# Halved loads for two more pairs, and a new order of all steps, in a fused linear-attention and gated-MLP kernel

## The chip, the cores and the metric

The kernel runs on one core of a Trainium2 chip. The metric is the device time of one execution in microseconds (us); lower is better. A core has five engines that run side by side: TensorE (PE in the profile) multiplies matrices, VectorE (DVE), ScalarE (ACT) and GpSimd (POOL) work on elements, and SyncE (SP) issues most transfers between the chip's main memory and the on-chip memory. TensorE writes to PSUM, a memory of eight banks. Each engine takes its instructions strictly in the order in which they were written.

## The reference

Inputs are `q`, `k`, `v`, `f_logit` of shape (4, 8, 768, 48) and two weight matrices (384 x 2048 and 2048 x 384), all in float32.

```python
f = 1.0 / (1.0 + np.exp(-f_logit))
for t in range(S):                       # S = 768
    state = f[:, :, t, :, None] * state + np.einsum('bhd,bhe->bhde', k[:, :, t], v[:, :, t])
    y[:, :, t] = np.einsum('bhd,bhde->bhe', q[:, :, t], state)
x = y.transpose(0, 2, 1, 3).reshape(3072, 384)
h = x @ w_in
out = (h * np.cos(h)) @ w_out
```

## The kernel before

The 3072 tokens are cut into 12 *pairs* of 256 tokens, three for each of the four batches. The recurrence is computed in chunks: within a chunk as masked scores, between chunks through a 48 x 48 state of each head. Each pair is a small graph of *steps*, named by kind, pair and part:

- `f k q v`: loads, issued by SP. A pair in `HALVES` loads f, k and q as two halves of four heads each (`f0.0`, `f0.1`, 192 KB apiece); any other pair loads them whole (384 KB). `w0.j` and `w1.j` load quarters of the two weight matrices (768 KB), and `wc` casts them to bfloat16.
- `ex ln cum eb ei`: the gate. ACT forms log(1 + exp(-f)), PE sums it over the tokens with a triangular matrix (`cum`), and ACT takes exp of the sums with both signs (`eb`, `ei`).
- `qm km`: q and k times these decays; `tq tk qkt`: their transposes, on PE with a copy out of PSUM by DVE or ACT (pairs 0 to 3), or as a transposing transfer by SP (pairs 4 to 11).
- `vb vt`: v as bfloat16, and a second copy of it laid out for the output blocks.
- `sc am`: scores on PE, and the mask on DVE. `ps st si sz`: the state's sum, its carry, and its decay. `y yi xe`: the output from scores and from the state, and its copy out of PSUM.
- `zX.i`: zeroing of a buffer. `zf0` and up: matmuls on a tile of zeros, which compute nothing that is used; their number is `ZEROS`.

Two neighbouring tokens share one partition, as the even and the odd *parity*. In a whole pair, POOL first adds the two parities' logarithms (`ad`), so that `cum` needs one sum for both, and corrects for the even parity afterwards with a separate gate: ACT makes it (`fx`, `fy`), and POOL multiplies it into q and k (`qa`, `ka`). In a pair of `HALVES`, `ln` writes both parities as bfloat16, and `cum` (L386) sums over both on PE with two masks, `incl` and `strict`, for each half of the heads; `ad`, `fx`, `fy`, `qa` and `ka` do not exist there, and `ex`, `ln`, `cum`, `eb` and `ei` exist once for each half:

```python
for z in xe:
    for x in xe:
        nc.tensor.matmul(o[:, :, HB * z:HB * z + HB], lhsT=strict if x > z and cut else incl,
                         rhs=w[:, x, :, 0:D].rearrange("p (u h) d -> p u h d", u=un),
                         start=(z == 0 and x == 0), stop=False)
```

The MLP runs over units of 256 tokens, one for each pair: `h` (first product, L634, in eight half steps of six matmuls that fill two PSUM banks each with its twin), `co` (cosine on ACT, L639), `g` (product on DVE, L616), `o` (second product, L650, four steps for each 128 tokens), `ot` (copy out of PSUM) and `out` (store).

Nothing decides the order at run time. The string `ORDER` lists every step in one sequence that a planner wrote ahead of time, each with an engine letter (T TensorE, S ScalarE, V VectorE, G GpSimd, Y SyncE) and the buffer slots or PSUM banks that it takes: `h0.10:T0` is the first half step of block 1 of unit 0, on TensorE, in the banks from 0 on. `emit` writes the steps in that sequence, and each engine gets its part of it as its queue. Semaphores between the engines follow from the data and from the reuse of slots and banks.

Of the kernel before, what the change touches and what calls it, by code (L numbers as in the profile page):

```python
# [55 lines left out]
tq3.1:T6 w1.1:Y2 tk3.1:T qkt3.1:S2 ka2:G qkt3.0:V3 o2.2:T1 g1.3:V o1.2:T7 km2.1:G0 v2:Y1 o0.2:T0
wc1.0:S km2.0:G o3.2:T6 w1.3:Y4 sc3.0:T2 sc3.1:T4 qa2:G am3.0:V0 o0.0:T f4:Y2 o3.0:T qm2.1:G
am3.1:V2 vb3:S2 o2.0:T qm2.0:G tk2.1:T2 vt3.3:S0 tq2.1:T tk2.0:T3 qkt2.1:V4 f5:Y1 tq2.0:T ps3.0:T4,5
qkt2.0:V0 ps3.1:T wc1.1:G o1.0:T sz3.01:V0 sc2.0:T2 sz3.00:V k5:Y0 am2.0:V1 vb2:G0 o3.1:T o2.1:T
vt2.2:S2 vt3.1:G vt3.2:G ps2.1:T4 ps2.0:T sc2.1:T2 k4:Y2 st2.00:V wc1.3:G o0.1:T am2.1:V3 o1.1:T  # L60
st3.10:V v4:Y2 vt2.1:G o1.3:T ex4:S st3.11:V vt2.0:G o3.3:T ot1:V0 ln4:S1 vt2.3:G q4:Y1 o0.3:T
sz2.00:V3 ex5:S st2.01:V ad4:G2 o2.3:T sz2.01:V fx4:S ot3:V1 q5:Y2 ln5:S0 vt3.0:G cum4:T4 ot2:V2
y2:T2,3 ei4:S2 yi2:T ad5:G2 fy5:S yi3:T6 f9:Y0 y3:T1 xe2.0:V2 fx5:S ka4:G xe2.1:V fy4:S cum5:T7
sz3.10:V1 ei5:S0 h2.11:T2 sz3.11:V ka5:G out2:Y eb5:S2 xe3.1:V1 h2.10:T eb4:S0 xe3.0:V km4.1:G2
h2.21:T6 ot0:V3 v5:Y1 h2.01:T4 km4.0:G co2.1:S2 h2.00:T h3.21:T0 qa4:G co2.0:S3 g2.1:V1 h3.20:T
f6:Y2 qm4.0:G h2.20:T co3.2:S1 g2.0:V h2.31:T2 qm4.1:G co2.2:S0 h2.30:T g3.2:V3 vb4:G2 tq4.1:Y0
h3.11:T4 co2.3:S2 qa5:G g2.2:V h3.10:T h3.31:T0 vt4.2:S0 vt4.3:G f7:Y1 g2.3:V co3.1:S3 h3.30:T
vt4.0:G km5.1:G0 o5.1:T7 co3.3:S1 g3.1:V tq4.0:Y1 o4.0:T6 qm5.1:G o5.2:T g3.3:V q6:Y0 qm5.0:G
ps4.0:T4,5 sc4.1:T2 ps4.1:T o5.3:T st4.00:V ex6:S vb5:G0 tq5.1:Y4 st4.01:V o4.1:T sz4.01:V3 km5.0:G
ln6:S0 sz4.00:V o5.0:T out1:Y st4.11:V zsz.2:G fx6:S o6.3:T0 am4.1:V2 k6:Y2 ex7:S vt5.1:G2 o6.1:T  # L70
vt5.3:G tq5.0:Y3 ln7:S1 st4.10:V ps5.1:T1 ad6:G1 ps5.0:T sc4.0:T2 sz4.10:V2 o4.2:T am4.0:V3 fx7:S
zqk.1:G v6:Y2 o4.3:T vt4.1:S vt5.0:G ot5:S0 cum6:T4 sz4.11:V ad7:G2 ot4:S2 yi4:T2,3 st5.01:V ei6:S0
y4:T sz5.01:V1 eb6:S1 vt5.2:G sc5.1:T6 st5.00:V xe4.1:S2 xe4.0:V cum7:T5 o6.2:T out4:Y am5.1:V1
# [699 lines left out]
```

## Time and profile before

| | |
|---|---|
| time, median of 3 runs | 179.11 us (179.11 to 179.7) |
| profiled execution | 179.25 us |
| span, first to last instruction | 177.4 us |
| busy: PE / DVE / ACT / POOL | 168.1 / 134.3 / 128.9 / 106.3 us |
| matmuls on zeros | 28, 9.8 us of PE's busy time |
| first matmul of the MLP | 23.95 us |
| last copy out of PSUM starts | 174.20 us |

The span runs from the program's first instruction to its last; what the profiled execution's own time has beyond it lies around the program. A busy share counts every instruction of an engine, the matmuls on zeros among them, so it is to be read together with what the instructions do. In group rows, the figures after the bar are the group's busy time, the mean duration of one instruction in ns, and the idle time of the engine just before them, with what ended it.

### The profile page before, as it was taken

What the parts mean: (1) busy time and instruction counts of PE and PEld (TensorE: products, weight loads), DVE (VectorE), ACT (ScalarE), POOL (GpSimd) and SP (SyncE); (2) the same over time, 40 slices, a digit from 0 to 9 for tenths busy, and PEclk for the clock granted to TensorE, in tenths of its full rate; (3) what the DMA queues carried; (4) which work ended last, traced back from release to release, by engine and by line L of the source; (5) the groups of instructions that cost most, each with busy time, mean ns of one, the idle gap of its engine ahead of it and who ended that gap; (6) DMA issues with size and microseconds to landing.
All of it is one profiled execution on the core that took longest, in us unless ns stands there. A gap on an engine that the chain in (4) does not pass through costs nothing.

```text
span 177.4 us, 5663 instructions
## 1 busy us (share of the span) xinstructions
PE 168.1 (95%) x2402; PEld 121.8 (69%) x2402; DVE 134.3 (76%) x201; ACT 128.9 (73%) x179; POOL 106.3 (60%) x134
## 2 busy tenths in 40 slices
PE   2897999999999999999999999999999999999992
PEld 0454678966678866788668786668866876888661
DVE  6139897989886999979798878677578897685721
ACT  3778898895769999889998879968855460485401
POOL 5245899999769999779767993529796000000000
PEclk9999999999999999999999999999999999999999
DMA  5999999999944699996999996976009602210103
GB/s 137 321 323 370 351 378 372 285 366 322 252 137 108 147 260 232 262 299 147 231 242 263 315 155 154 204 199 193 0 0 167 166 0 89 81 60 0 44 4 133
DMA packets 74394, 34.45 MB, mean 194 GB/s; under 512 B 67457, under 2 KB 72833, under 8 KB 74369
## 3 DMA queue, kind: packets, MB, share of 16 engines
q1 hardware_dynamic: 73024, 33.50, 72.3%
q10 hardware_dynamic: 1344, 0.59, 1.1%
q8 instruction: 19, 0.31, 0.8%
q14 instruction: 7, 0.05, 0.1%
HBM read 25.17 MB, written 4.72 MB: 168 GB/s over the span
## 4 chain that ended last, share of the span: by engine, by line
PE 85%; DVE 7%; POOL 3%; ACT 3%; issue 1%; POOLq 0%; DVEq 0%
PE ps L650 36%; PE ps L634 34%; PE ps L572 5%; PE ps L472 4%; PE ps L386 2%; PE ps L512 2%; DVE qk L416 2%; PE ps L451 1%; DVE qkt L196 1%; DVE incl L217 1%; ACT bj L403 1%; DVE sz L544 1%; PE ps L277 1%; DVE x L196 1%; DVE am L494 1%
## 5 line engine op out<-in xcount | busy, mean ns | idle before, releaser
L616 DVE TENSOR_TENSOR g<-ps,co 128x1024 bf16<-128x1024 f32 x48 | 57.8, 1222 | 15.4 <-ACT co L639 13.4
L650 PE MATMUL ps<-w_out_bf,g 128*128 128x384 bf16 x384 | 67.3, 326 | 0.0
L634 PE MATMUL ps<-x,w_in_bf 128*128 128x256 bf16 x576 | 66.3, 273 | 0.2 <-DVE x L196 0.2
L639 ACT ACTIVATE co<-ps,halfpi 128x1024 bf16<-128x1024 f32 x48 | 52.7, 1113 | 16.9 <-PE ps L634 13.0
L634 PEld LDWEIGHTS <-w_in_bf 128*128 128x128 bf16 x576 | 55.5, 98 | 8.5 <-issue 0.4
L650 PEld LDWEIGHTS <-g 128*128 128x128 bf16 x384 | 36.2, 98 | 22.4 <-DVE g L616 0.2
L494 DVE TENSOR_TENSOR am<-ps,pmask 128x1024 bf16<-128x1024 f32 x24 | 28.6, 1218 | 5.8 <-PE ps L472 4.5
L416 POOL TENSOR_TENSOR qk<-k,bi 128x384 bf16<-128x384 f32 x20 | 19.8, 1000 | 0.6
L416 POOL TENSOR_TENSOR qk<-q,b 128x384 bf16<-128x384 f32 x20 | 19.7, 999 | 0.7
L373 POOL TENSOR_TENSOR sp<-ls 128x384 bf16<-128x384 f32 x10 | 10.0, 998 | 13.3 <-ACT ls L346 7.1
L196 POOL COPY vt<-vb 64x384 bf16<-64x384 bf16 x32 | 16.0, 501 | 2.6 <-ACT vb L196 1.0
L196 ACT COPY ot<-ps 128x384 f32<-128x384 f32 (+1 forms) x10 | 4.5, 461 | 12.7 <-PE ps L650 6.9
L544 DVE TENSOR_TENSOR sz<-ps,b 64x192 bf16<-64x192 f32 x32 | 11.3, 354 | 1.3 <-PE ps L512 0.4
L196 DVE COPY ot<-ps 128x384 f32<-128x384 f32 (+1 forms) x16 | 8.1, 514 | 5.5 <-PE ps L650 5.5
L360 POOL TENSOR_TENSOR k<-k,f 128x384 f32<-128x384 f32 x10 | 10.0, 1002 | 3.4 <-ACT ot L196 3.3
L538 DVE TENSOR_TENSOR ps<-ps,sz 64x192 f32<-64x192 f32 x28 | 10.3, 366 | 1.8 <-PE ps L512 0.8
L342 ACT ACTIVATE f<-f 128x768 f32<-128x768 f32 (+1 forms) x14 | 10.3, 746 | 1.0 <-DMA f<-in_f_logit_dram 0.8
L277 PE MATMUL ps<-zero 128*128 128x512 bf16 x28 | 9.8, 445 | 1.2 <-DVE zero L203 1.2
L350 POOL TENSOR_TENSOR q<-f,q 128x384 f32<-128x384 f32 x10 | 10.0, 1000 | 1.3 <-ACT f L353 1.3
L196 ACT COPY vt<-vb 64x384 bf16<-64x384 bf16 x16 | 8.1, 508 | 2.4 <-POOL vb L196 2.1
L472 PE MATMUL ps<-qkt 48*64 48x128 bf16 (+1 forms) x320 | 8.8, 219 | 0.7 <-DVE qkt L196 0.6
L196 POOL CAST vb<-v 128x768 bf16<-128x768 f32 x8 | 6.6, 824 | 4.7 <-DMA v<-in_v_dram 3.4
(66 smaller groups left out, 167.9 us busy)
## 6 DMA issues: line engine op xcount, KB each, us to landing
v<-in_v_dram SPq DMA_DIRECT2D x12, 384.0 KB, 4.9
out_dram<-ot SPq DMA_DIRECT2D x22, 192.0 KB, 3.3
f<-in_f_logit_dram SPq DMA_DIRECT2D x10, 384.0 KB, 5.1
k<-in_k_dram SPq DMA_DIRECT2D x10, 384.0 KB, 5.6
q<-in_q_dram SPq DMA_DIRECT2D x10, 384.0 KB, 5.7
g<-in_moe_w_in_dram SPq DMA_DIRECT2D x4, 768.0 KB, 8.8
g<-in_moe_w_out_dram SPq DMA_DIRECT2D x4, 768.0 KB, 7.2
q<-in_q_dram SPq DMA_DIRECT2D x4, 192.0 KB, 3.7
```

Of the source, the lines that this page charges most:

```text
L196: (nc.scalar.copy if e == "ACT" else eng(e).tensor_copy)(out=o, in_=i)
L277: G.step(f"zf{i}", ("PE",), lambda e, dump=dump: nc.tensor.matmul(dump.ap, lhsT=zero[:, 0:128], rhs=zero, start=True, stop=True), writes=[ ...
L342: nc.scalar.activation(out=flat(t.ap), in_=flat(t.ap), func=AF.Exp, scale=-1.0)
L416: G.step(f"{nm}{n}.{u}", ("POOL", "DVE") if cut else ("POOL",), lambda e, u=u, j=j, src=src, dec=dec: eng(e).tensor_mul(out=qkp[u][j].ap[: ...
L472: nc.tensor.matmul(o[t0:t1, r, 2 * a + g, :].rearrange("p (e n) -> p e n", e=2), lhsT=wide[s, t0 // 64, :] if turned else wide[s].rearrang ...
L494: G.step(f"am{n}.{u}", ("DVE",), lambda e, u=u, sc=sc: nc.vector.tensor_mul(out=am[u].ap.rearrange("p r b n -> p (r b) n"), in0=sc.ap.rear ...
L538: nc.vector.tensor_add(out=view()[s], in0=view()[s], in1=S0.ap[s, :, r, :])
L544: eng(e).tensor_mul(out=new.ap[s, :, r, :].rearrange("p (u a) n -> p u a n", u=2), in0=view()[s].rearrange("p (u a) n -> p u a n", u=2), i ...
L616: nc.vector.tensor_mul(out=o.rearrange("p b (n e) -> p b n e", e=2), in0=ph.ap.rearrange("p (b e n) -> p b n e", e=2, n=64), in1=co.ap.rea ...
L634: nc.tensor.matmul(ph.ap[:, i * T:(i + 1) * T].rearrange("p (g t) -> p g t", t=C), lhsT=w_in_bf[:, kk, f0:f0 + 128], rhs=xa[:, :, kk, :], ...
L639: G.step(f"co{m}.{j}", ("ACT",), lambda e, ph=ph, co=co: nc.scalar.activation(out=co.ap, in_=ph.ap, func=AF.Sin, bias=halfpi), reads=[ph], ...
L650: nc.tensor.matmul(po.ap[:, 0:DM], lhsT=gT.ap[:, j, i * C:(i + 1) * C], rhs=w_out_bf[:, j, :], start=(po.first and j == 4 * s), stop=(po.f ...
```

## The change

Three things are edited: two constants and the whole of `ORDER`.

- `HALVES` goes from pairs 0, 1 to pairs 0, 1, 2, 3. Pairs 2 and 3 lose `ad`, `fx`, `fy`, `qa` and `ka`; their `ex`, `ln`, `cum`, `eb`, `ei` and the loads of f, k and q come in two halves. Steps `qm` and `km` of these pairs may run on DVE as well as on POOL.
- `ZEROS` goes from 28 to 17.
- `ORDER` is a new plan of all 904 steps (909 before). Engines, slots and banks of steps are chosen anew too. `f0.0` and `f0.1`, which ACT issued, are issued by SP, the former as the very first load; `f0.1` is the third.

```diff
-HALVES = (0, 1)
+HALVES = (0, 1, 2, 3)
-ZEROS = 28
+ZEROS = 17
-f1.1:Y2 f0.1:S1 zf0:T5 v0:Y0 f0.0:S zf1:T0 q0.0:Y1 zqk.2:G k1.1:Y1 zqk.0:G zvt.2:G k0.0:Y2 ex1.1:S
-zsp.2:V zsz.0:V f1.0:Y ln1.1:S2 zvt.0:V zsp.1:V cum1.1:T2 k0.1:Y zf2:T3 q0.1:Y ei1.1:S0 vb0:G0
-zf3:T1 ex0.1:S zf4:T4 f2:Y0 ex0.0:S vt0.2:G0 zf5:T6 ln0.0:S1 eb1.1:S0 cum0.0:T0 v1:Y1 ln0.1:S zf6:T5
-zf7:T7 ei0.0:S1 zf8:T6 zf9:T6 cum0.1:T7 km0.0:G0 zf10:T4 f3:Y1 ei0.1:S zf11:T3 eb0.0:S1 zsz.3:G
-tk0.0:T4 zf12:T6 eb0.1:S vt0.3:G km0.1:V ps0.0:T2,0 vt0.1:S k1.0:Y ex1.0:S ps0.1:T zf13:T6 sz0.00:V0
-q1.1:Y0 vt0.0:S zf14:T6 zf15:T3 sz0.01:V zf16:T5 q1.0:Y st0.11:V zf17:T1 tk0.1:T6 ex2:S km1.1:V2
-zf18:T1 w0.1:Y0 qm0.0:V tk1.1:T3 ln2:S1 zf19:T7 qm0.1:V tq0.0:T zf20:T5 vb1:S1 qkt0.0:V2 w0.0:Y3
-ad2:G1 ln1.0:S sz0.11:V3 sc0.0:T4 tq0.1:T st0.10:V zsz.1:G ex3:S cum2:T2 am0.0:V1 w0.2:Y1 cum1.0:T7
-vt1.1:G2 zf21:T1 ei1.0:S vt1.2:G zf22:T1 zf23:T1 ei2:S1 qkt0.1:V0 zf24:T4 km1.0:G zf25:T5 eb1.0:S
-sz0.10:V ln3:S0 sc0.1:T6 ps1.1:T0,4 am0.1:V0 zf26:T1 eb2:S0 k3:Y2 ad3:G1 ps1.0:T fx3:S si1.0:T
-tk1.0:T1 fx2:S qm1.0:V yi0:T5 qm1.1:G y0:T6 sz1.01:V1 tq1.0:T xe0.1:S2 cum3:T7 sz1.00:V w0.3:Y2
-xe0.0:S qkt1.0:V0 tq1.1:T fy2:S zf27:T2 wc0.1:G qkt1.1:V1 eb3:S1 sc1.0:T0 ei3:S0 am1.0:V3 yi1:T3,2
-vt1.0:S sc1.1:T6 q3:Y2 si1.1:T vt1.3:G am1.1:V0 h0.10:T0 wc0.0:S h0.11:T sz1.10:V1 sz1.11:V y1:T
-w1.2:Y4 h0.01:T6 xe1.1:V0 wc0.2:G xe1.0:V h0.00:T co0.1:S3 k2:Y1 h1.01:T2 ka3:G h1.21:T4 fy3:S
+f0.0:Y0 zf0:T0 v0:Y0 zf1:T3 f0.1:Y zqk.2:G k0.0:Y0 f1.1:Y1 f1.0:Y q0.0:Y0 ex0.0:S zsz.2:V zvt.2:V
+k0.1:Y zsp.2:V zvt.0:V ln0.0:S2 zqk.1:V q0.1:Y vb0:G1 cum0.0:T5 q1.1:Y1 ex0.1:S vt0.0:G2 zf2:T4
+f3.1:Y2 ln0.1:S zf3:T0 vt0.2:G ei0.0:S0 f2.1:Y0 zf4:T2 eb0.0:S0 km0.0:V2 cum0.1:T1 k1.1:Y1 ex1.1:S
+zsp.1:V tk0.0:T3 v1:Y0 eb0.1:S qm0.0:G zf5:T4 zf6:T2 ei0.1:S zf7:T5 ex1.0:S km0.1:V zsz.0:G k1.0:Y
+tq0.0:T ln1.1:S2 ps0.0:T2,5 qkt0.0:V1 ln1.0:S q1.0:Y cum1.1:T0 vt0.3:G zsz.3:V zf8:T6 vt0.1:S f2.0:Y
+qm0.1:V ps0.1:T ei1.1:S0 zf9:T7 w0.1:Y2 tk0.1:T1 sz0.01:V2 ex3.1:S cum1.0:T7 sz0.00:V eb1.1:S1
+tq0.1:T zf10:T6 st0.11:V ei1.0:S f3.0:Y zf11:T0 qm1.1:G2 st0.10:V zf12:T4 ex2.1:S sz0.10:V0 w0.0:Y0
+ln2.1:S2 sz0.11:V tq1.1:T4 ln3.1:S1 km1.1:V sc0.0:T2 km1.0:G w0.2:Y4 qkt0.1:S0 zf13:T0 am0.0:V0
+cum2.1:T5 tk1.1:T eb1.0:S zf14:T6 w0.3:Y1 zf15:T0 vb1:S2 qkt1.1:V2 sc0.1:T6 qm1.0:G zf16:T2 am0.1:V3
+ei2.1:S1 tk1.0:T1 ps1.0:T4,3 ex2.0:S ps1.1:T vt1.2:G0 si1.0:T eb2.1:S0 tq1.0:T vt1.3:G sz1.01:V3
+yi0:T2 ln2.0:S y0:T0 sz1.00:V qkt1.0:V0 sc1.1:T6 xe0.1:S2 q3.0:Y2 wc0.1:G xe0.0:S am1.1:V2 sc1.0:T4
+q3.1:Y ex3.0:S cum2.0:T2 cum3.1:T1 ln3.0:S am1.0:V0 vt1.1:G h0.10:T6 ei2.0:S w1.2:Y3 eb2.0:S vt1.0:G
+si1.1:T cum3.0:T0 ei3.1:S0 sz1.11:V2 wc0.0:G y1:T4,5 ei3.0:S sz1.10:V yi1:T eb3.0:S1 h0.11:T eb3.1:S
+xe1.0:V1 k3.1:Y2 xe1.1:V h0.01:T0 zqk.0:V wc0.2:G h0.00:T k2.0:Y0 co0.1:S3 h1.01:T4 k3.0:Y h1.00:T
+co0.0:S2 g0.1:V4 wc0.3:G h1.21:T2 w1.0:Y2 co1.0:S0 h1.20:T g0.0:V qm3.0:G0 h1.11:T6 q2.1:Y0 h1.10:T
...
```

More of the change, by code (lines that the diff above doesn't have):

```diff
@@ L56 @@
[L56 to L73, printed above, removed]
@@ L115 @@
-ot21:S2 out21:Y
+f0.0:Y0 zf0:T0 v0:Y0 zf1:T3 f0.1:Y zqk.2:G k0.0:Y0 f1.1:Y1 f1.0:Y q0.0:Y0 ex0.0:S zsz.2:V zvt.2:V
[3 more added lines that the diff above has]
+tq0.0:T ln1.1:S2 ps0.0:T2,5 qkt0.0:V1 ln1.0:S q1.0:Y cum1.1:T0 vt0.3:G zsz.3:V zf8:T6 vt0.1:S f2.0:Y
@@ new lines @@
+h1.31:T2 km3.1:G co0.3:S3 h0.20:T v2:Y2 tk3.1:T6 g0.3:V km3.0:G co0.2:S0 h1.30:T tq3.0:T7 zsz.1:G
+tk3.0:T co1.3:S2 g0.2:V tq3.1:T k2.1:Y o3.2:T4 wc1.0:G qkt3.1:S3 o2.2:T5 f4:Y1 g1.3:V o0.2:T1
+qkt3.0:S1 km2.0:G2 o0.0:T qm2.0:V v3:Y1 o1.2:T0 qm2.1:G sc3.0:T2 sc3.1:T6 wc1.1:S am3.0:V0 o3.0:T
+w1.3:Y3 o1.0:T vb2:G2 am3.1:V2 f5:Y0 o2.0:T vt2.1:G0 o3.1:T km2.1:V vt2.0:G q4:Y0 tq2.0:T6 ex4:S
+tk2.0:T tk2.1:T2 qkt2.0:V4 tq2.1:T o1.1:T vt2.3:S v4:Y0 qkt2.1:V2 vb3:G1 ln4:S0 sc2.0:T6 am2.0:V3
+vt3.3:G2 ps3.1:T3,2 ps3.0:T fy4:S o0.1:T vt3.1:S k4:Y2 sz3.00:V1 o2.1:T wc1.3:G vt3.2:S sz3.01:V
@@ L116 @@
+out21:Y
 """
```

99 lines of the change are left out of this document (55 added, 44 removed).

## The prediction

> **What bounds the kernel now.** I read the page first (span, busy shares, chain), then the busy time by stretches, then the chain in order of time, then the start instruction by instruction. The page, with its shares of the chain by engine:
>
> ```profile
> span 177.4 us, 5663 instructions
> PE 168.1 (95%) x2402; PEld 121.8 (69%) x2402; DVE 134.3 (76%) x201; ACT 128.9 (73%) x179; POOL 106.3 (60%) x134
> PE 85%; DVE 7%; POOL 3%; ACT 3%; issue 1%; POOLq 0%; DVEq 0%
> ```
>
> TensorE is busy for 95% of the span, but part of that is filler on the tile of zeros. The stretches (length, then busy time of PE, PEld, DVE, ACT, POOL) and the chain in order of time (start, length) say where it does needed work; the first of these rows are the matmuls on zeros alone, the next three are all instructions:
>
> ```profile
> 0.00:10.00 10.00, 4.23 (x10) 0.94 (x10) 0.27 (x1) 1.00 0.90 240
> 10.00:20.00 10.00, 5.17 (x18) 1.42 (x17) 0.00 (x0) 1.00 1.10 357
> 25.98:174.20 148.22, 147.93 (x2089) 109.64 (x2088) 117.36 (x159) 108.67 (x143) 90.70 (x108) 1.00 0.70 175
> 11.03:25.05 14.02, 12.51 (x243) 7.99 (x241) 12.82 (x22) 12.85 (x25) 9.36 (x11) 1.00 1.08 358
> 6.39:23.06 16.67, 14.95 (x243) 8.85 (x244) 10.83 (x20) 14.14 (x31) 10.05 (x14) 1.00 1.10 347
> ...
> 23.95 1.47 PE ps L634 x12
> 25.42 0.56 PE ps L572 x32
> 25.98 9.28 PE ps L634 x84
> ...
> 174.20 0.48 ACT ot L196
> ```
>
> Read this as three parts. From 25.98 us, where step h0.01 starts (h0.10, h0.11 and y1 come just before it), to 174.20 us PE stops for only 148.22 - 147.93 = 0.29 us. The tail, from 174.20 to 177.4, is 3.2 us of copy and store. The first 26 us are the filling of the pipeline: DVE is busy for 12.82 of 14.02 us there, ACT for 14.14 of 16.67, and PE's apparent load is padded with 9.4 us of zeros. So only the first part can become shorter, and the middle can only keep its 0.29 us of stalls or get more.
>
> Call A the time at which h0.01 starts. In both orders the same 266 TensorE steps stand from h0.01 to the end, and ahead of it the same steps but for the sums of pairs 2 and 3 and the fillers. With an unchanged middle, the end moves by exactly what A moves.
>
> **The change part by part.** The durations that I use (group rows: busy, mean ns), then the moments of the start:
>
> ```profile
> L342 ACT ACTIVATE f<-f 128x768 f32<-128x768 f32 x10 | 8.4, 838 | 0.1
> L346 ACT ACTIVATE sp<-f 128x384 bf16<-128x384 f32 x4 | 2.1, 519 | 0.1
> L403 ACT ACTIVATE bj<-ps 128x384 f32<-128x384 f32 x4 | 2.0, 490 | 2.8 <-PE ps L392 2.8
> L356 ACT ACTIVATE f<-ls 128x384 f32<-128x384 f32 x10 | 5.1, 521 | 0.1
> L196 ACT CAST vb<-v 128x768 bf16<-128x768 f32 x4 | 3.3, 824 | 0.0
> L196 ACT COPY qkt<-ps 128x1024 bf16<-128x1024 bf16 x1 | 1.0, 1003 | 0.0
> L494 DVE TENSOR_TENSOR am<-ps,pmask 128x1024 bf16<-128x1024 f32 x24 | 28.6, 1218 | 5.8 <-PE ps L472 4.5 <-PE ps L572 1.2
> L196 DVE COPY qkt<-ps 128x1024 bf16<-128x1024 bf16 x7 | 4.7, 684 | 0.4 <-PE ps L451 0.4
> L544 DVE TENSOR_TENSOR sz<-ps,bb 64x192 bf16<-64x192 f32 x8 | 2.8, 353 | 0.6 <-PE ps L512 0.5
> L416 POOL TENSOR_TENSOR qk<-q,b 128x384 bf16<-128x384 f32 x20 | 19.7, 999 | 0.7
> L196 POOL CAST w_in_bf<-g 128x1536 bf16<-128x1536 f32 x3 | 4.4, 1461 | 0.1
> ...
> 3.96 0.52 ACT L342 ACTIVATE f<-f 128x384 f32<-128x384 f32 x1 [0.80 <-DMA f<-in_f_logit_dram]
> 5.83 1.87 PE L277 MATMUL ps<-zero 128*128 128x512 bf16 x4
> 8.85 0.49 ACT L403 ACTIVATE bj<-ps 128x384 f32<-128x384 f32 x1 [0.18 <-PE ps L392]
> 12.11 1.25 PE L277 MATMUL ps<-zero 128*128 128x512 bf16 x5
> 16.35 0.33 PE L386 MATMUL ps<-sp,incl 128*128 128x384 bf16 x1
> 16.62 0.24 PE L386 MATMUL ps<-sp,incl 128*128 128x192 bf16 x1
> 17.05 1.37 PE L277 MATMUL ps<-zero 128*128 128x512 bf16 x5
> 24.83 1.28 ACT L639 ACT_TABLE_LOAD   x1
> 26.12 1.11 ACT L639 ACTIVATE co<-ps,halfpi 128x1024 bf16<-128x1024 f32 x1
> ```
>
> *Pairs 2 and 3 by halves.* Removed per pair: three POOL products (ad, qa, ka), 3 x 1.0 us, so 6 us in all; POOL is idle 40% of the span and ends no part of the middle, so I count nothing. On ACT, ex and ln as wholes (0.84 each), fx and fy (0.52 each), one ei and one eb (0.49 each), 3.7 us, become four halves of 0.52 and four of 0.49, 4.0 us: +0.3 us per pair, in the start. On PE one whole sum took 16.35 to 16.62 = 0.27 us; a half with both parities 16.62 to 17.05 = 0.43, so 0.86 per pair: +1.2 us for both. They stand before A, where 11 fillers go (0.25 us each by 12.11's row), 2.8 us; the cover is PE's idle time there. If that were gone, they would cost 1.2. DVE gets two of the products qm, km (about 0.6 each) in the middle, where it is busy for 117 of 148 us: nothing.
>
> *Loads.* The bytes stay; 200 KB pieces replace wholes, and SP issues 9 more entries (f +4, k +2, q +2, out +1), among them f0.0 and f0.1 that ACT issued before. Moved past SP's queue, f0.1 lands third. The landings below are issue time plus time to landing, in the order: first two f halves (issued at 0.74), second f half and v0 (1.25), k0.0 (3.1), w0.0 (12.9).
>
> ```profile
> DMA to landing us min/median/max: 3.2/3.4/3.5
> DMA to landing us min/median/max: 4.9/5.0/5.1
> DMA to landing us min/median/max: 4.9/4.9/4.9
> DMA to landing us min/median/max: 8.1/8.1/8.1
> ```
>
> So 384 KB had landed at 4.25 us, 960 at 6.3, 1536 (with k0.0) at 8.0, and w0.0, byte position 5376 KB, at 21.0. In the new order f0.1 ends at 768 KB: by interpolation 5.6 us (an estimate). q0.0 takes the place of 1536 KB: 8.0 us. w0.0 stays at 5376 KB: 21.0. Two entries can hold SP up: f2.1 needs f0.1 read by ln0.1 (6.7 below) and v1 needs v0's slot free (cast before 7 us); both are issued about 4 us before they land, as the rows show, so the loads in flight cover that.
>
> *The new order up to A.* ex0.0 starts at 3.96 as now, waiting for the same first load. ex0.1 and ln0.1 follow f0.1: 5.6 + 2 x 0.52 = 6.7; ei0.0 ends at 7.1 to 7.2, where it ended at 8.85 + 0.49 = 9.34 before. qm0.0 (POOL, 1.0) waits for q0.0: 8.0 to 9.0. Then tq0.0, ps0.0, cum1.1 on PE, some 1.4 us with fillers, and ei1.1, ex3.1, eb1.1 on ACT (1.5): eb1.1 ends at 12.0, or 12.8 if no ACT instruction overlaps the one before. qm1.1 on POOL (1.0), then tq1.1 and sc0.0 on PE (0.8 with the handoffs): am0.0 starts at 14.0 to 14.9. From here DVE is a straight row of am0.0, qkt1.1, am0.1, sz1.01, sz1.00, qkt1.0, am1.1, am1.0: 4 x 1.22 + 2 x 0.68 + 2 x 0.35 = 6.9 us, plus up to 0.5 of waiting for sc0.1: 20.9 to 22.4. y1 and yi1 then take 0.9 us and h0.11 0.66 (6 x 9.28/84): A by this path is 22.5 to 24.0.
>
> Two other conditions hold h0.01. It takes PSUM banks 0 and 1, which hold cum3.0 and cum3.1 until eb3.0 and eb3.1 have read them, and these are the last of 35 ACT instructions from ex0.1 on. Their durations add to 18.4 us (14 x 0.52, 16 x 0.49, vt, vb, qkt, two xe). In the stretch 6.39:23.06 ACT ran 29 instructions whose own durations add to 16.2 in 14.14 us, so overlap saves 13%: 16.0 us. From 5.6 that is 21.6 without a wait and 24.2 with the 2.5 us of waiting of that stretch. And it needs wc0.0: 21.0 + 1.46 = 22.5. So A lies between 22.5 and 24.65 (24.0 or 24.2 plus late handoffs); I take 23.7, just past the middle, because three paths meet there. That is 2.3 us earlier than 25.98.
>
> *After A.* Banks come free through co and g. Before, the first co started at 26.12; now the table load (1.28) and co0.1 (1.11) follow eb3.1, which ends near 22.9: 25.3. PE needs that bank six half steps (3.9 us) after A, at 27.6, and g0.1 ends at about 25.3 + 1.3 = 26.6: it fits. Pair 3's k comes late in the queue: behind w0.0 (21.0) stand w0.2, w0.3, q3, w1.2 and k3.1, 2880 KB, at the 358 GB/s of the stretch 11.03:25.05 some 8.2 us, so it lands near 29.2, k3.0 1.1 later, and POOL forms km3.1 and km3.0 by 31.6; PE asks for them at A + 8.5 = 32.2. That is little slack, so I give the middle 0.4 us more stalls than its 0.29 (bounds: -0.29, and +1.5, five times the present sum).
>
> *Tail and ends.* The last steps are the same copy and store by ACT and SP: 3.2 us. One store moves from ACT to SP, off the last chain: nothing.
>
> *The sum.* 23.7 + 148.2 + 0.4 + 3.2 = 175.5 us of span. The profiled execution took 179.25 for 177.4, so 1.85 lies around the span: 177.35; it was 0.14 above the median, 179.11. Forecast **177.2**.
>
> **A rule that speaks against it.** The four fillers at 5.83 took 0.47 us each, the five at 12.11 0.25: PE runs at about half speed until some 10 us, though the clock column reads 1.00. With 11 fillers fewer it could fall back. Were it slow for the first 3.4 us of the h steps, 31 matmuls of 0.11 us would take twice that: +1.7, so 178.9. My walk leaves no pause over 1 us after 5 us, so I give this 7 in 100. The Trainium skill, "TensorE: Matmul & The Clock Gate", section "What's actually happening", says that the slow state is the default and that an idle window of about 3.4 us restores it; the slow fillers agree with the first, and no run here shows the second.
>
> **Rivals.** (1) Everything overlaps: A = 22.5, no new stall: 174 of span, 175.5. For it: ACT's rows overlap when nothing is awaited. Against: the w0.0 transfer is then in the path as well. 12 in 100. (2) The start stays hidden behind ACT: the queue keeps today's waits and the handoffs of the extra halves, A = 25 to 26: 178.5 to 179.5. For it: ACT gains 6 instructions before A. 10 in 100. (3) Slower: the same queue as a block. Without overlap, and with 0.1 us at each of 35 handoffs, eb3.1 ends at 5.6 + 18.4 + 3.5 = 27.5; banks 0 and 1 are not free before, A = 27.6, 1.6 later than now: 180.7. It decides once eb3.1 ends after 26.9. Against: 13% overlap in the present rows. 7 in 100; another 4 for stalls of 3 us or more in the middle, from late halves of pair 3. (4) That the sums are not moved is excluded: the steps stand in the order.
>
> **How the numbers follow.** A measurement of this kernel tells about 0.5%, 0.9 us, from no change. Forecast 60 and rival 1's 12 are faster: 0.72. Rival 2's 10 and the clock's 7 are the same: 0.17. Slower: 0.11. Range 175.4 (rival 1) to 179.3 (A = 24.65 with 1.5 us of stalls); it leaves out about 2 in 10 with the slower cases. The forecast's own range is 176 to 178.2.
>
> **What would show it.** Right: ei0.0 ends near 7.2, am0.0 starts near 14.5, h0.01 near 23.7; the zeros take under 7 us of PE; from A to the last matmul about 148.5 us. Wrong: an idle time of PE before h0.01 put to ACT's eb3 or to the cast of w0.0; waits of PE on POOL's km3 near 32 us; fillers or h matmuls at double length after 12 us; or a middle over 150 us.

## The result and the profile after

The changed kernel took 177.74 us (median of 8 runs, 176.86 to 180.01) against 179.49 us (8 runs, 178.74 to 180.15) for the kernel before, run in turn. The ratio is 0.9883, with a 95% interval from 0.9852 to 0.9913: about 1.2% faster. Forecast were 177.2 us against 179.11, a ratio of 0.989. The medians are over all 8 runs and alone give 0.990; the ratio leaves out the two slowest runs of the changed kernel (179.6 and 180.01), which lie over 1.5% above its fastest.

The profiled execution took 178.54 us, so it is one of the longer ones. Its page, in the order of the lines shown of before:

```profile
span 176.8 us, 5711 instructions
PE 166.5 (94%) x2411; PEld 122.0 (69%) x2413; DVE 129.2 (73%) x195; ACT 130.2 (74%) x187; POOL 102.4 (58%) x130
PE 74%; DMA 13%; POOL 5%; ACT 3%; SPq 2%; issue 1%; POOLq 0%; ACTq 0%
```

The shares of the chain say at once that in this execution the end hangs on other things: DMA, which was not in that row before, holds 13% of it, and DVE, which held 7%, is gone. The stretches (length, then busy time and count of PE, PEld, DVE, ACT, POOL); the first two rows are the matmuls on zeros alone, the others all instructions:

```profile
0.00:10.00 10.00, 3.96 (x8) 0.82 (x8) 0.27 (x1) 1.00 0.88 236
10.00:20.00 10.00, 2.36 (x7) 0.78 (x9) 0.00 (x0) 1.00 1.06 315
24.00:173.18 149.18, 147.87 (x2089) 109.47 (x2087) 112.62 (x151) 111.30 (x149) 88.96 (x106) 1.00 0.73 181
5.49:23.80 18.31, 16.51 (x312) 11.28 (x313) 13.38 (x24) 15.94 (x35) 10.92 (x16) 1.00 1.08 330
14.62:22.05 7.43, 6.72 (x152) 4.92 (x153) 6.69 (x8) 5.99 (x14) 5.56 (x8) 1.00 1.04 357
```

Three numbers account for the span. Step h0.01 starts at 24.00 us (A), where it started at 25.98. From there to the start of the last copy out of PSUM, right behind PE's last matmul, it is 149.18 us, where it was 148.22, and the busy time in it is the same: 147.87 and 147.93. So PE's stalls in the middle grew from 0.29 to 1.31 us. The tail, 173.18 to 176.8, is 3.6 us instead of 3.2. In this execution that leaves -1.98 + 0.96 + 0.4 = -0.6 us of span.

What releases h0.01 is read from the chain in order of time, up to the first long row of h:

```profile
1.79 3.68 DMA f<-in_f_logit_dram
...
5.49 0.53 ACT f L342
...
9.71 6.33 DMA k<-in_k_dram
...
16.18 1.01 POOL qk L416
...
23.34 9.34 PE ps L634 x84
```

The row at 23.34 begins with h0.11, six matmuls before h0.01. The start hangs on two transfers: f0.1, in flight from 1.79 to 5.47, and k1.0, issued at 9.71 and landing at 16.04 after 6.33 us. DVE's instructions in order of time (start, length, operation, and in brackets the idle time before with its releaser), first of before and then of after, show where the earlier start comes from:

```profile
11.03 0.78 DVE L416 TENSOR_TENSOR qk<-k,bj 128x384 bf16<-128x384 f32 x1 [5.95 <-ACT bj L403]
...
16.55 1.22 DVE L494 TENSOR_TENSOR am<-ps,pmask 128x1024 bf16<-128x1024 f32 x1
...
22.69 2.35 DVE L494 TENSOR_TENSOR am<-ps,pmask 128x1024 bf16<-128x1024 f32 x2
```

```profile
6.98 0.56 DVE L416 TENSOR_TENSOR qk<-k,bj 128x384 bf16<-128x384 f32 x1 [2.41 <-ACT bj L403]
...
9.17 0.85 DVE L416 TENSOR_TENSOR qk<-k,bj 128x384 bf16<-128x384 f32 x1 [1.49 <-DMA k<-in_k_dram]
...
14.62 1.22 DVE L494 TENSOR_TENSOR am<-ps,pmask 128x1024 bf16<-128x1024 f32 x1 [0.15 <-PE ps L472]
...
19.69 2.36 DVE L494 TENSOR_TENSOR am<-ps,pmask 128x1024 bf16<-128x1024 f32 x2
```

The release in brackets is the point. The row at 11.03 is km0.1 of before, for which DVE stood idle until ACT had made ei0.1; km0.0 ran on POOL there. In after DVE forms both: km0.0 at 6.98, right behind ei0.0, and km0.1 at 9.17, 1.86 us earlier than before although it waited 1.49 us for its load. That lead is kept: am0.0 starts 1.93 us earlier. It even grows, and the last two masks end at 22.05 instead of 25.04, 2.99 us earlier: one transposed copy (qkt0.1) and one product (qm1.0) of DVE's row in before run on ACT and POOL in after. But A gains only 1.98 us. From 17.23 us on the chain of after lies on PE alone, up to h0.01 and beyond: behind the masks PE still has the rest of cum3.0, y1, yi1 and h0.11 to do; in before only the rest of h0.11 and y1 were left. So in after the masks are no longer the last thing that A waits for; PE's own work is.

The new stalls of PE in the middle are two, in its instructions in order of time, and each has its releaser:

```profile
45.96 0.81 PE L650 MATMUL ps<-w_out_bf,g 128*128 128x384 bf16 x4 [0.87 <-POOL w_out_bf L196]
...
61.73 0.42 PE L472 MATMUL ps<-qkt 48*64 48x128 bf16 x16 [0.40 <-DMA qkt<-qk]
```

The first waits for the cast of w1.3 on POOL, which itself waited for the load. The second waits for a transposing transfer.

### The profile page after: what moved, and what is told of

Its sections match the earlier page's. It is cut to its first block, busy times and chain, and to the rows that moved or that the text cites. A ratio compares the mean times of both kernels' runs of the same rounds, so it can differ in the third digit from the quotient of the medians.

```text
span 176.8 us, 5711 instructions
## 1 busy us (share of the span) xinstructions
PE 166.5 (94%) x2411; PEld 122.0 (69%) x2413; DVE 129.2 (73%) x195; ACT 130.2 (74%) x187; POOL 102.4 (58%) x130
## 4 chain that ended last, share of the span: by engine, by line
PE 74%; DMA 13%; POOL 5%; ACT 3%; SPq 2%; issue 1%; POOLq 0%; ACTq 0%
PE ps L634 31%; PE ps L650 30%; PE ps L572 5%; DMA g<-in_moe_w_out_dram 4%; DMA k<-in_k_dram 4%; PE ps L472 3%; POOL qk L416 3%; DMA qkt<-qk 3%; DMA f<-in_f_logit_dram 2%; SPq L309 2%; PE ps L512 2%; PE ps L386 1%; POOL k L360 1%; POOL w_out_bf L196 1%; ACT co L639 1%
## 5 line engine op out<-in xcount | busy, mean ns | idle before, releaser
L196 ACT COPY ot<-ps 128x384 f32<-128x384 f32 (+1 forms) x16 | 7.5, 469 | 15.8 <-PE ps L650 10.3
L416 POOL TENSOR_TENSOR qk<-k,bi 128x384 bf16<-128x384 f32 x16 | 15.9, 1000 | 0.7
L416 POOL TENSOR_TENSOR qk<-q,b 128x384 bf16<-128x384 f32 x16 | 15.9, 999 | 0.4
L342 ACT ACTIVATE f<-f 128x384 f32<-128x384 f32 (+1 forms) x16 | 10.8, 682 | 4.5 <-DMA f<-in_f_logit_dram 4.5
L373 POOL TENSOR_TENSOR sp<-ls 128x384 bf16<-128x384 f32 x8 | 7.9, 999 | 5.8 <-ACT ls L346 5.8
L196 ACT CAST x<-ps 128x384 bf16<-128x384 f32 x13 | 5.9, 482 | 6.9 <-PE ps L572 6.9
L350 POOL TENSOR_TENSOR q<-f,q 128x384 f32<-128x384 f32 x8 | 8.0, 999 | 4.5 <-DMA out_dram<-ot 2.8
L544 DVE TENSOR_TENSOR sz<-ps,b 64x192 bf16<-64x192 f32 x26 | 9.2, 353 | 0.7 <-PE ps L512 0.2
L386 PE MATMUL ps<-sp,incl 128*128 128x192 bf16 (+1 forms) x32 | 7.1, 288 | 2.4 <-DVE qk L241 2.4
L472 PEld LDWEIGHTS <-qkt 48*64 48x64 bf16 (+1 forms) x320 | 5.7, 104 | 4.7 <-issue 2.2
```

The source lines that it names most:

```text
L196: (nc.scalar.copy if e == "ACT" else eng(e).tensor_copy)(out=o, in_=i)
L342: nc.scalar.activation(out=flat(t.ap), in_=flat(t.ap), func=AF.Exp, scale=-1.0)
L416: G.step(f"{nm}{n}.{u}", ("POOL", "DVE") if cut else ("POOL",), lambda e, u=u, j=j, src=src, dec=dec: eng(e).tensor_mul(out=qkp[u][j].ap[: ...
L472: nc.tensor.matmul(o[t0:t1, r, 2 * a + g, :].rearrange("p (e n) -> p e n", e=2), lhsT=wide[s, t0 // 64, :] if turned else wide[s].rearrang ...
L544: eng(e).tensor_mul(out=new.ap[s, :, r, :].rearrange("p (u a) n -> p u a n", u=2), in0=view()[s].rearrange("p (u a) n -> p u a n", u=2), i ...
```

## The experiments

Ratios are against the kernel before, run alongside. Edits are against the changed kernel but for e3, which edits the kernel before. Removing or adding lines of `ORDER` or code moves the line numbers below it by a few: in e2 by 5, in e3 by 6 against before, in e4 by 3. A new `zf` step has `ZEROS` raised with it.

**e1: the changed kernel again.** No edit.

> The changed kernel once more, unaltered, to see which of the waits of its first profile belong to it. My account of the first profile: the MLP's long stretch (A, the start of h0.01) begins at 24.0 us instead of 25.98, and 1.0 us of this is lost again in two TensorE waits, 0.87 us near 45 us (the cast of the last quarter of w_out, whose load had landed late) and 0.40 us near 61.5 us (a transposing transfer). If these waits are chance (a load that landed late in that execution), they are gone here, the span is near 175.5 us and the ratio to before is 0.988 or a little less. If they belong to the order, they stand at the same steps again with the same 0.5 to 1.5 us, and A is at 24.0 again (23.7 to 24.3).

177.54 us; ratio 0.9879 (0.9839 to 0.9918). Its profiled execution took 177.16 us for a span of 175.4. The middle as a stretch, then rows of POOL, DVE and PE in order of time:

```profile
23.23:171.79 148.56, 147.82 (x2089) 109.29 (x2087) 113.31 (x151) 111.34 (x149) 88.84 (x106) 1.00 0.73 183
```

```profile
14.21 1.05 POOL L416 TENSOR_TENSOR qk<-k,bj 128x384 bf16<-128x384 f32 x1 [0.41 <-DMA k<-in_k_dram]
...
18.93 2.34 DVE L494 TENSOR_TENSOR am<-ps,pmask 128x1024 bf16<-128x1024 f32 x2
...
45.09 1.14 PE L650 MATMUL ps<-w_out_bf,g 128*128 128x384 bf16 x6 [0.59 <-POOL w_out_bf L196]
```

Here k1.0 landed early enough for its product to start at 14.21 instead of 16.18; the last pair of masks starts at 18.93 instead of 19.69, and A is 23.23 instead of 24.00. am0.0 starts at 14.62 in both, so what parts these two is when k1.0 lands. It is not the only thing that moves A. In e6 and e10 below, whose start is the same, am0.0 starts at 14.08 and 14.57 and A is 22.7 and 23.2, which is 8.6 us behind it, as in e1 (in after it is 9.4): where k1.0 is in time, A hangs on am0.0.

The wait for w1.3's cast is there again (0.59 us), and the one at 61.7 us is not. Neither is fixed by the order: e4 and e8, with the same middle, wait 0.63 and 0.80 us for this cast, while e2 and e9 do not wait for it at all and lose 1.2 and 0.8 us to transposing transfers near 69 us. This execution: -2.75 + 0.34 + 0.4 = -2.0 us of span.

**e2: two fillers in the new order.**

```diff
-ZEROS = 17
+ZEROS = 2
   (zf2 to zf16 taken out of ORDER)
```

> The changed kernel with zf2 to zf16 left out, so that TensorE has only the two matmuls on zeros ahead of its first sum. Theory of the path: A is set by the needed steps on ACT, POOL, PE and DVE in turn, and fillers only fill waits, so A stays at 24.0 within 0.5 us and the ratio to before stays at 0.985 to 0.992. Theory of the clock (rival in the prediction): with too few matmuls TensorE stays at, or falls back to, half speed; then its matmuls between 10 and 20 us show twice their length, the first 3.4 us of h steps take 1.7 us more, and the ratio is 0.997 or above. Theory that fillers lie in the way: A is 0.5 us or more earlier than 24.0.

178.77 us; 0.9948 (0.9914 to 0.9982): about half of the gain is lost. A is 24.35, and neither of the two main theories is met: the matmuls before 14 us are slow, the first h steps are not. PE's instructions in order of time, then two stretches:

```profile
12.32 0.59 PE L446 MATMUL ps<-ident,qk 128*128 128x128 bf16 x4
...
14.19 0.40 PE L446 MATMUL ps<-ident,qk 128*128 128x128 bf16 x4 [1.27 <-POOL qk L411]
...
18.55 1.07 PE L567 MATMUL ps<-am,vt 128*32 128x128 bf16 x32
...
22.71 0.63 PE L567 MATMUL ps<-am,vt 128*32 128x128 bf16 x32
```

```profile
12.00:16.00 4.00, 2.69 (x43) 2.05 (x41) 3.40 (x6) 3.78 (x8) 2.52 (x3) 1.00 1.11 360
16.00:20.00 4.00, 3.67 (x107) 2.93 (x102) 3.31 (x6) 2.31 (x6) 3.71 (x5) 0.57 1.02 354
```

Rows of the same form and count are to be compared: four transposes took 0.59 us at 12.32 and 0.40 at 14.19, 32 output matmuls 1.07 us at 18.55 and 0.63 at 22.71. PE was slow until about 14 us, fast, and slow again for most of 16 to 20, which the granted clock (0.57) shows too. Fillers are not ballast here; taking them out costs, and the gain does not come from there being fewer.

**e3: two fillers in the order before.**

```diff
-ZEROS = 28
+ZEROS = 2
   (zf2 to zf27 taken out of ORDER)
```

> The kernel before with zf2 to zf27 left out, nothing else altered: the only part of the change that can be made by itself without a new order. In the trace of before the chain passes 1.24 us of fillers at half speed (8.81 to 10.05) between ln0.1 and cum0.1. If the gain of the change came from having fewer fillers, A moves from 25.98 to 24.8 or below and the ratio is 0.990 to 0.993. If it came from the order of the needed steps, cum0.1 comes earlier but DVE's row of work (12.8 us busy of 14.0) still ends near 25 us: A at 25.2 to 26, ratio 0.995 to 1.0. If fillers are needed for the clock: A later than 26.5, ratio 1.003 or more.

182.06 us; 1.0148 (1.0114 to 1.0182). The same eight score matmuls twice, then the stretch that ends between them:

```profile
23.84 0.61 PE L466 MATMUL ps<-qkt 48*128 48x128 bf16 x8
...
25.14 0.40 PE L466 MATMUL ps<-qkt 48*128 48x128 bf16 x8
```

```profile
20.00:24.00 4.00, 4.00 (x95) 3.17 (x89) 3.77 (x6) 2.51 (x7) 3.94 (x4) 1.00 1.05 356
```

The eight take 0.61 us and then 0.40: the start of the old order stays slow up to 24 us, and PE becomes fast behind a stretch in which it was busy for 4.00 of 4 us. The clock column reads 1.00 all the time: of this kind of slowness it shows nothing. A is 27.85 us. By the medians of runs made side by side the fillers are worth 2.5 us to the old order (182.06 against 179.56) and 1.2 us to the new one (178.77 against 177.54).

**e4: a delay just before h0.01.**

```diff
-xe1.0:V1 k3.1:Y2 xe1.1:V h0.01:T0
+xe1.0:V1 k3.1:Y2 xe1.1:V zf17:T2 zf18:T2 zf19:T2 zf20:T2 zf21:T2 h0.01:T0
```

> The changed kernel with five more matmuls on zeros directly ahead of h0.01, 1.1 us of TensorE time at the length of a filler at full speed (0.22 us). It asks whether the end follows A one for one, as the prediction's sum assumes. If TensorE bounds the whole middle: A at 25.1, the end 1.1 us later, ratio 0.994 against 0.988 for the changed kernel. If the middle is bound by transfers that arrive when they arrive (the waits near 45 and 61.5 us), the delay is taken out of these waits and the ratio stays at 0.988 to 0.990, with the waits gone from the trace.

177.88 us; 0.9924 (0.989 to 0.9958). PE's fillers and the matmuls of h0.01 behind them:

```profile
22.58 1.24 PE L274 MATMUL ps<-zero 128*128 128x512 bf16 x4
23.66 1.58 PE L631 MATMUL ps<-x,w_in_bf 128*128 128x256 bf16 x13
```

The delay is 1.08 us. Against e1, run alongside, the ratio rose by 0.0045, or 0.8 us, but the intervals overlap, and the ratio lies between the two that were expected. The traces say more: from h0.01 (23.82) to the last copy (172.17) it is 148.35 us here, 148.56 in e1 and 149.18 in after, and A differs by up to 0.8 us between them. The middle is no shorter for the delay, so the delay went to the end in full, as the sum took it. (Without it A would have been about 22.6.)

**e5: pairs 2 and 3 whole again, in the new order.** By hand: the loads and the `ex`, `ln`, `cum`, `eb` and `ei` of these pairs become whole steps at the place of one of their halves; `ad`, `fx`, `fy`, `qa` and `ka` come back; qm2.0 and km2.1 go to POOL. The core of the edit:

```diff
-HALVES = (0, 1, 2, 3)
+HALVES = (0, 1)
-... ln3.1:S1 km1.1:V sc0.0:T2 km1.0:G w0.2:Y4 ... sc0.1:T6 qm1.0:G ...
+... ln3:S1 km1.1:V sc0.0:T2 km1.0:G ad2:G2 w0.2:Y4 ... sc0.1:T6 ad3:G1 qm1.0:G ...
```

> The new order with pairs 2 and 3 whole again (HALVES = (0, 1)): their ad, fx, fy, qa and ka are put back beside the steps of the same pair, the load, ex, ln, cum, eb and ei of the halves are joined at the place of one half, and qm2.0 and km2.1 go back to POOL. It asks what the halves are worth inside this order. The prediction counted POOL's relief (6 us) as nothing. If that is right, TensorE's end moves by no more than 0.5 us, ratio 0.985 to 0.991 (ACT even has 0.7 us less in the start). The rival: POOL is the engine that the halves relieve; it is busy for 13.5 of the 16 us from 24 to 40, so 6 us more do not fit, the q and k products of pair 3 come after 33 us, TensorE waits there by 2 us or more, and the ratio is 1.0 or above.

180.0 us; 1.0029 (1.0007 to 1.005): the whole gain is gone. A is 27.1. Its start in order of time, and PE's slow stretch:

```profile
14.71 1.23 DVE L494 TENSOR_TENSOR am<-ps,pmask 128x1024 bf16<-128x1024 f32 x1 [0.41 <-PE ps L472]
...
16.98 1.95 POOL L373 TENSOR_TENSOR sp<-ls 128x384 bf16<-128x384 f32 x2
...
18.88 0.99 POOL L416 TENSOR_TENSOR qk<-q,bb 128x384 bf16<-128x384 f32 x1
...
19.93 0.61 PE L451 MATMUL ps<-ident,qk 128*128 128x128 bf16 x4 [1.53 <-POOL qk L416]
...
22.41 2.36 DVE L494 TENSOR_TENSOR am<-ps,pmask 128x1024 bf16<-128x1024 f32 x2 [0.69 <-PE ps L472]
```

```profile
20.00:25.00 5.00, 4.96 (x80) 3.60 (x81) 3.05 (x3) 3.11 (x8) 4.77 (x7) 0.50 1.06 366
```

Two readings. Up to am0.0 (14.71, against 14.62 in after) nothing is lost: the 1.9 us by which am0.0 is earlier than before need no halving of pairs 2 and 3, the order gives them. Behind it the last masks start at 22.41 instead of 19.69. The two sums on POOL (1.95 us) stand ahead of qm1.0, PE waits 1.53 us for that, and from then on it runs at half speed (the granted clock of the stretch is 0.50). That alone is a large part of the loss: the 4.96 us of PE's work in the stretch would take about half as long at full speed (an estimate), and A is 3.1 us later than in after. How much of the rest is the whole steps and how much their places, which no planner chose, it cannot say. So e5 does not show what the halves are worth.

**e9: two more products on POOL in the start.** The same load as the two `ad`, but on a scratch buffer and with the halves kept:

```diff
-sc0.1:T6 qm1.0:G
+sc0.1:T6 pd0:G pd1:G qm1.0:G
```

> The changed kernel with two more POOL products (128x384 float32 on a scratch tile, 1.0 us each, read by nobody) directly ahead of qm1.0, where the whole pairs had the sums ad2 and ad3. With whole pairs A had come at 27.1 instead of 23.2 to 24.0. If POOL's two sums in the start are what the halves save, A moves by 1 to 2 us here (24.5 to 26) and the ratio is 0.994 to 1.0, which is most of the way to the 1.003 of the whole pairs. If the loss with whole pairs came from elsewhere (TensorE at half speed there, or my placing of its other steps), A stays within 0.5 us of 23.2 to 24.0 and the ratio stays at 0.987 to 0.990.

177.5 us; 0.9897 (0.9844 to 0.995), not to be told from after. POOL in order of time:

```profile
14.45 2.05 POOL L233 TENSOR_TENSOR scr<-scr 128x384 f32<-128x384 f32 x2
16.46 1.00 POOL L416 TENSOR_TENSOR qk<-q,bb 128x384 bf16<-128x384 f32 x1
```

The products take 2.05 us of POOL between km1.0 and qm1.0, as the two `ad` do in e5. Here km1.0 started at 13.50, and qm1.0 has to wait for its gate on ACT anyway: in e1 it starts at 15.61, here at 16.46, and A is 23.4 (23.2 in e1). In e5 km1.0 started at 16.02 only, behind a late k1.0 (SP issued it at 10.94, in after at 9.71, since f2 and f3 stood ahead of it as wholes), and the same two us went onto the path. So POOL's two sums alone are not what the halves save in a start in which k1.0 comes early; where it comes late, as in e5, they cost.

**e10: four such products in the middle**, ahead of qm3.0, km3.1, km2.0 and qm2.1.

```diff
-g0.0:V qm3.0:G0 ... h1.31:T2 km3.1:G ... qkt3.0:S1 km2.0:G2 ... o1.2:T0 qm2.1:G
+g0.0:V pd0:G qm3.0:G0 ... h1.31:T2 pd1:G km3.1:G ... qkt3.0:S1 pd2:G km2.0:G2 ... o1.2:T0 pd3:G qm2.1:G
```

> The same kind of product four times, one each ahead of qm3.0, km3.1, km2.0 and qm2.1, where the whole pairs had qa3, ka3, ka2 and qa2: 4 us more of POOL from 26 to 37 us, after the start. The prediction counted POOL's relief in the middle as nothing. If so, A and the ratio stay (0.987 to 0.990), and TensorE's waits after A stay the one near 45 us. The rival: POOL was busy 13.5 of the 16 us from 24 to 40, 4 us do not fit, TensorE waits for km3 or for the casts of w_out by 1 us or more more than before, ratio 0.993 or above.

177.68 us; 0.9914 (0.988 to 0.9948). The stretch 24 to 40 us here, PE's one stall in it, and the same stretch in e1:

```profile
24.00:40.00 16.00, 15.47 (x144) 11.86 (x142) 13.15 (x12) 14.23 (x15) 15.24 (x17) 1.00 1.08 335
```

```profile
32.37 0.40 PE L451 MATMUL ps<-ident,qk 128*128 128x128 bf16 x4 [0.53 <-POOL qk L416]
```

```profile
24.00:40.00 16.00, 15.95 (x147) 12.20 (x146) 13.30 (x12) 14.27 (x15) 13.69 (x14) 1.00 1.08 330
```

POOL is busy for 15.24 of 16 us, and PE loses 0.53 at the very place that the prediction named (the transposes of km3). The wait for w1.3's cast near 45 us is not there, as it is not in e9, and the profiled span is 175.1, no longer than e1's. In that execution POOL's relief in the middle is worth at most half a microsecond. The ratio lies between the two that were expected, and its interval holds both.

**e6: w1.3 earlier in SP's queue**, ahead of f4 and v3, to take away the wait at 45 us.

```diff
-o2.2:T5 f4:Y1 ... v3:Y1 ... o3.0:T w1.3:Y3
+o2.2:T5 w1.3:Y3 f4:Y1 ... v3:Y1 ... o3.0:T
```

> The changed kernel with one entry of SP's queue moved: the load of the last quarter of w_out (w1.3) goes ahead of f4 and v3 (768 KB, 2.3 us at 340 GB/s). In three executions TensorE waited 0.6 to 0.9 us near 45 us for the cast of this quarter, whose load landed at 43.5 to 44.3. If the place in the queue of transfers makes this wait, it is gone, w1.3 lands near 41.5, and the ratio falls by 0.003 (0.985 against 0.988), provided that f4 and v3, 2 us later, hold up nothing: v3's cast is the first that could. If the load is late for another cause (SP held up by a wait), its landing stays after 43 us and nothing changes.

178.18 us; 0.9929 (0.9887 to 0.9972). POOL's cast of v3 and PE's product behind it:

```profile
42.41 0.82 POOL L196 CAST vb<-v 128x768 bf16<-128x768 f32 x1 [3.50 <-DMA v<-in_v_dram]
...
43.28 0.44 PE L512 MATMUL ps<-vb,qk 64*64 64x48 bf16 x32 [2.00 <-POOL vb L196]
```

The wait at 45 us went, and v3, now later, put a wait of 2.00 us at 41.28 in its place. The entry moved and the loads behind it paid; ahead of the moved entry SP itself waited 0.8 us for a cast on POOL.

**e11: f4 later instead**, behind w1.3.

```diff
-o2.2:T5 f4:Y1 g1.3:V ... am3.1:V2 f5:Y0
+o2.2:T5 g1.3:V ... am3.1:V2 f4:Y1 f5:Y0
```

> The changed kernel with f4 moved behind w1.3 in SP's queue, v3 left ahead of it. Moving w1.3 ahead of both had taken its wait near 45 us away and put one of 2.0 us at 41.3 in its place, since v3, 2.2 us later, was what ps3.1 needed. If both loads stand in one queue of transfers at its full rate, v3 and w1.3 now land 1.2 us earlier each (39 and 42.5), the waits at 41 and 45 both go, f4 (needed by ACT alone) lands 2 us later, and the ratio falls by 0.003 to 0.985. If ACT, which waits for f4 in its own queue ahead of vt2.3, vt3.1 and vt3.2, passes the delay on, a wait appears at y3 or ps3 and the ratio stays at 0.988 or rises.

179.61 us; 0.9983 (0.9942 to 1.0024). ACT's first step on f4, and PE's longer wait:

```profile
43.21 0.84 ACT L342 ACTIVATE f<-f 128x768 f32<-128x768 f32 x1 [4.48 <-DMA f<-in_f_logit_dram]
...
49.61 0.61 PE L572 MATMUL ps<-am,vt 128*32 128x128 bf16 x29 [1.67 <-ACT ot L196]
```

ACT waited 4.48 us for f4 with its later work queued behind, and PE lost 1.67 us at 47.9 and another 0.73 at 45.9, where the sum of pair 4's decays waited for it. So f4 had no slack for such a delay. Not all of the delay is the transfer of w1.3: SP first waited 1.7 us for POOL before it could issue w1.3, with f4 queued behind it, and issued f4 at 36.39 only.

**e7: f0.1 second in SP's queue**, ahead of v0, since the chain begins with its landing.

```diff
-f0.0:Y0 zf0:T0 v0:Y0 zf1:T3 f0.1:Y
+f0.0:Y0 zf0:T0 f0.1:Y v0:Y0 zf1:T3
```

> The changed kernel with f0.1 issued second, ahead of v0, where it stands third. The profile shows ACT waiting 0.9 us for f0.1 before ex0.1 (5.49 us) at the head of the chain. The prediction held that the start is one chain from this landing on. If so, f0.1 lands near 4.3, ex0.1 starts about 1 us earlier, and A (23.2 to 24.0 in two executions) moves up by 0.3 to 1.0 us, as far as the later landings (q0.0 at 8.1 to 8.4, k1.0 at 14 to 16) let it; ratio 0.983 to 0.986. If those later landings bind the start, not this one, A stays and the ratio stays at 0.988.

178.68 us; 0.993 (0.9891 to 0.997): no gain. Its profiled execution took 180.28 us, 1.6 above the median, so only the first rows of ACT are used:

```profile
4.30 0.51 ACT L342 ACTIVATE f<-f 128x384 f32<-128x384 f32 x1
...
7.84 0.52 ACT L342 ACTIVATE f<-f 128x384 f32<-128x384 f32 x1 [1.61 <-DMA f<-in_f_logit_dram]
```

ACT's ex0.1 starts at 4.30 instead of 5.49, without a wait; the next half that ACT needs, f1.1, then makes it wait 1.61 us. It took the first transfer off the path and put the next one there. The ratio is above both that were expected.

**e8: five fillers at the very beginning**, behind zf1, where PE waits for the first data.

```diff
-zf1:T3 f0.1:Y
+zf1:T3 zf17:T5 zf18:T1 zf19:T6 zf20:T4 zf21:T7 f0.1:Y
```

> The changed kernel with five more matmuls on zeros after zf1, in the 2.4 us in which TensorE waits for its first sum (2.2 to 4.6 us); 22 instead of 17. Leaving fillers out kept TensorE at half length of time per matmul till 14 us in the new order and till 24 us in the old. If sustained work is what brings the full speed, it comes 2 us earlier here (near 7.5 us instead of 9.9), cum0.1, tk0.0 and zf5 to zf7 take half the time, and A is 0.3 to 0.8 us earlier: ratio 0.984 to 0.986. If the speed comes at a time that the program does not set, or A hangs on the landings, nothing changes (0.988).

176.89 us; 0.9858 (0.9814 to 0.9901). The first two rows of PE:

```profile
1.19 3.17 PE L277 MATMUL ps<-zero 128*128 128x512 bf16 x7 [1.19 <-DVE zero L203]
4.50 0.24 PE L386 MATMUL ps<-sp,incl 128*128 128x192 bf16 x1
```

PE is at full speed from its first needed sum (0.24 us; in after 0.32 at 4.60, and slow until some 9.7 us). A is 23.3 all the same, as in e1, and the wait near 45 us is there with 0.80. It is the lowest median of all, but its interval overlaps that of after, and no earlier A stands behind it: a better version is not shown. This A hides something, though. ex0.1 waited 1.78 us for f0.1 and started at 6.24 us, in e1 at 5.58; from there to am0.0 it took 8.52 us, in e1 9.04. So in these traces, one execution each, early full speed looks worth some 0.5 us of the start, and a later landing of f0.1 took it back. The new order can have it without more fillers: in e6 three of them at 8.09 us took 0.87 us, where the same three at 8.15 took 1.48 in e1, and am0.0 started at 14.08.

**e12: the edits of e8 and e11 together.**

> The move of f4 and the five early fillers together, as a version that may beat both kernels. The early fillers brought full speed at 4.4 us and left A at 23.3: nothing to expect of them but a steadier start. Expected ratio: that of the moved f4, within 0.002; TensorE's first sum at full speed (0.24 us a matmul of 192 columns instead of 0.32).

179.13 us; 0.9968 (0.9936 to 1.0). A was 22.7, with ex0.1 at 5.62 and am0.0 at 14.13, and the two waits of e11 stayed (0.52 and 1.68 us): the late f4 has its price behind this start too. The first sum took 0.32 us, not the 0.24 that were expected; the matmuls from 4.81 us on are at full speed.

## Why the prediction was right, point by point

**A.** Forecast 23.7 within 22.5 to 24.65; measured 24.00 and 23.23 (e1). The steps on the way came close: ei0.0 ended at 6.95 (7.1 to 7.2 forecast), f0.1 landed at 5.47 (5.6), eb1.1 was done in time for qm1.1 at 12.79, and am0.0 started at 14.62 (14.0 to 14.9). DVE's row from there to the end of the last mask took 7.43 us with 6.69 busy (6.9 and up to 0.5 of waiting). The queue of ACT, 5.49 to 23.80, took 18.31 us, 35 instructions in 15.94 busy: the 16.0 with overlap were right, and so was the 2.5 us of waiting as an upper end. The zeros took 6.32 us (under 7). The three paths do meet: in after eb3.1 ended at 23.80 and the cast of w0.0 at 23.38, both within 0.7 us of A, though each 0.9 us later than forecast (22.9 and 22.5). co0.1, forecast to end at 25.3, ended near 26.2 for that reason; PE did not wait for it. Two things were not foreseen. One is k1.0: the walk let am0.0 to am1.0 hang on DVE alone, while POOL waited 2.38 us ahead of km1.0 for a load that is in none of its terms, and this moves A between after and e1. The other is that PE's own work, not DVE's masks, holds A at the end. The upper end of 24.65 is not worked out: the walk's 24.0 and 24.2 are, the late handoffs added to them have no row.

**The middle.** Forecast 0.4 us of new stalls, measured 1.02 in the profiled execution and 0.45 in e1 (148.56 - 147.82 = 0.74 against 0.29). The size holds, within the bound of 1.5; the place does not, so that the size came close is luck. The prediction looked at km3 near 32 us, where after has no stall. What stalled was the cast of w1.3 at 45 us, or in e2 and e9 transposing transfers near 69 us, of which it said nothing. e6 and e11 show why it is not simply removed: loads fill the queue there, SP itself waits for buffers, and each of the two exchanges made another load late, by 2 us and more of PE's time.

**The tail.** Forecast as unchanged 3.2 us; measured 3.6 in after and in e1 (171.79 to 175.4). "One store moves from ACT to SP, off the last chain: nothing" is the step that was mis-sized, by 0.4 us. The moved store now stands just ahead of the last one in SP's queue, but it does not hold that one up: the last store is issued 0.5 us behind the start of the last copy in both kernels (173.68 in after, 174.7 before). The 0.4 us lie behind that issue, where SP's waits at the program's end add up to 2.3 us in after and 1.8 in before; why is open.

**The sum.** Forecast 175.5 us of span; measured 176.8 in after (A +0.3, the middle +0.6, the tail +0.4) and 175.4 in e1, where A is 0.5 early and makes up for the tail. That e1 meets the number so closely is luck; that the gain is what A gains, less what the middle takes back, is not.

**POOL's 6 us counted as nothing.** For the middle e10 bears it out: four products more cost at most 0.5 us of PE. For the start, e9 says that 2 us more of POOL are nearly free while k1.0 comes early. But e5, where the halving is undone, lost all the gain behind am0.0, a large part of it to PE's half speed. What halves bring there (sums on PE without a step on POOL in between, ACT's shorter pieces, places that can be planned, or fewer pauses of PE and with them the full clock) stays open.

**Fillers.** That 11 fewer save time was not claimed, and e2 and e3 show the reverse: fillers earn 1.2 us in the new order and 2.5 in the old. The clock rival was right as a mechanism (e2, e5), and did not happen in after: its h matmuls run at 0.111 us each (9.34 us for 84), as before. Its price holds as 1.7 us, but not by way of the 31 matmuls: in 3.4 us at half speed half of them get done, and the other half is the 1.7. The Trainium skill, "TensorE: Matmul & The Clock Gate", section "What's actually happening", says that about 3.4 us of sustained work releases the throttle and that an idle window of the same length restores it. e8 and e3 agree with the first half: full speed behind 3.17 us of fillers, and in e3 only behind 4 us without a pause. The second half fits e2 less well: PE fell back at 16 us, and of the 4 us before that it had worked 2.69, with no pause longer than 1.27.

**The other rivals.** That everything overlaps (A = 22.5) was nearly reached in e6 and e12 (22.7), with k1.0 early and am0.0 at 14.1; the waits in their middles kept the time well above 175.5. Stalls of 3 us or more in the middle did not come (1.31 in after). That ACT hides the gain, or that its queue ends after 26.9, is out: eb3.1 ended at 23.80.

## What to carry to other kernels

When one engine runs almost without a gap from some point to the end of the pipeline's filling (in before DVE, to the last mask), look at what it waits for just ahead of that point: here 5.95 us for the gate of the pair that comes first, and an earlier load with another order released 1.9 us of it. Then ask which engine is next: here the masks came 2.99 us earlier, A only 1.98, since PE's own work took over. Before one entry of a full queue of loads is moved up, ask who needs those that it passes, and whether the issuing engine can issue it at once: the two exchanges tried around 45 us made a wait of 2.0 us and two of 2.4 us together out of one of 0.6. Matmuls on zeros are to be judged by the length of equal matmuls behind them, not by their share of busy time.
